# Quadrant products for the third batch of a fused attention and two-layer MoE kernel, with two engines' order written by hand from an earlier point

## The chip, the cores and the metric

One core of a Trainium2 chip runs the whole program. The metric is the device time of one execution in microseconds (us); lower is better. Where a median of runs is given, it is the median of three executions.

## The reference, cut to what matters

```python
attn_out = _attn_ref(q, k, v)                  # 4 batches, 8 heads, 576 tokens, head size 64; windows of 32 keys
x = attn_out.transpose(0, 2, 1, 3).reshape(4 * 576, 512)
h = np.maximum(np.maximum(x @ w1, x @ w2), x @ w3)   # 512 -> 768, three products and their maximum
x = h @ w_out                                         # 768 -> 512
logits = x @ w_gate                                   # gate, then a normalisation over tokens and experts
for e in range(8):
    out += P[:, e:e + 1] * (np.maximum(x @ w1[e], 0.0) @ w2[e])
```

Every product is done in float32 precision out of three passes: each operand is split into a high part and a low part (a copy on ScalarE, then a subtraction on VectorE or GpSimd), and high by high, low by high and high by low are summed.

## The kernel before, in words

The first half of the program works through the four batches (numbered 0 to 3). For each batch it does attention, then the "upper projections" (`x @ w1`, `x @ w2`, `x @ w3` and their maximum, rows 0 to 5 of the list `WORK`, as in "2.0" to "2.5"), then the lower projection ("2.out"). While TensorE multiplies for one batch, the attention of the next but one or next is slipped in. The list `WORK` is cut into units: six for each upper row, eight for each lower projection. Batch 1's rows 1.0 to 1.3 are units 56 to 79, "1.out" is 80 to 87, batch 2's rows are 88 to 123, "2.out" is 124 to 131 and batch 3's rows 132 to 167. After each unit `hooks(unit)` runs whatever the tables at the top of the file place there: `BEGIN` says in which unit each of four attention passes of a batch starts (each pass is two heads), and `LATE`, `PARTS` and `STAGES` say how many units later its steps come. Steps are named by letters: `S` the scores (TensorE), `Ma`, `Mb` the mask and the maximum (VectorE), `X` the exponentials (ScalarE), `Ra`, `Rb` the division (VectorE, then GpSimd), `T`, `E` the transposes and their evacuation, `V` the product with the values, `H`, `L` the evacuation of that product.

Upper projections come in two forms. `up` takes each of the 36 pieces of a batch (two halves of the 576 tokens, 18 column blocks) as 12 matmuls of 288 columns, 432 in all. `up_quads`, used for batch 3 alone, takes two column blocks and both token halves together as seven products of half the depth (Strassen's scheme in Winograd's form): nine such sets of 7 products of 6 matmuls, 378 in all. It needs sums of weight quadrants (`sums_w1`: four VectorE additions of 128x256 per set, fetched raw and stored to `wsf`), sums of the input's quadrants (`make_quad`: seven splits, four of them after a subtraction), and three more additions per set to put the results together (`result`). The sets go in groups of two; the fifth group has one.

The kernel keeps the split weights of the first two batches in DRAM (`wsp`), from where `up_quads` loads three quadrants as they are (`more_w1`, "A1" and "A2"); "S" loads the sums, "X" and "Y" split them.

What sets the order of instructions: TensorE's order is that of the code throughout. ScalarE's and VectorE's order is that of the code from "1.out" on, and before that a scheduler chooses it. GpSimd's and SyncE's order is the scheduler's. SyncE (SP) issues nearly all the DMAs, one after the other; each waits there until the buffer that it writes is free.

Of the kernel before, what the change touches and what calls it, by code (L numbers as in the profile page):

```python
# [9 lines left out]
F32 = mybir.dt.float32  # L10
# [7 lines left out]
B, H, S, D = 4, 8, 576, 64  # L18
# [5 lines left out]
    "2.0 2.1 2.2 2.3 2.4 2.5 2.out 3.0 3.1 3.2 3.3 3.4 3.5 3.out"  # L24
).split()

BEGIN = {2: (48, 60, 67, 71), 3: (91, 98, 105, 112)}
SUMS = (86, 89, 93, 96, 100, 103, 107, 110, 114)
WEIGHTS = 78
FIRST = {118: "S", 120: "A1", 121: "A2", 122: "X0", 123: "X1", 126: "Y0", 127: "Y1"}  # L30
LATE = {
    0: "S Ma", 1: "Mb", 2: "X0", 3: "X1", 4: "X2", 5: "X3", 6: "X4", 7: "Ra Rb", 8: "W",
    10: "T0 E0 T1 E1", 11: "T2 E2", 13: "V0 H0", 14: "V1 H1",
}
QUAD = {125: ("B11",), 126: ("T1",), 128: ("T2",), 129: ("B21",), 130: ("T3",), 132: ("B22",), 133: ("T4",)}
EARLY = {
    135: "X", 141: "d1", 143: "d3", 157: "d2", 159: "d4", 160: "w0", 165: "w1", 166: "A1.0", 167: "A2.0",
    168: "T2 s0", 169: "T1 S12.0", 170: "T3 S34.0", 171: "T4 A1.1", 172: "s1 A2.1", 173: "S12.1", 174: "S34.1",
}
PARTS = {  # L40
    0: "S Ma Mb X0", 1: "X1 X2", 2: "X3 X4 Ra Rb", 6: "W", 8: "T0 E0 T1 E1", 9: "T2 E2", 11: "V0 H0 L0 V1 H1 L1",
}
STAGES = {0: "S Ma Mb Xe Ra Rb", 6: "W", 8: "T0 E0 T1 E1", 9: "T2 E2", 11: "V0 H0 L0 V1 H1 L1"}


ORDER = (
# [25 lines left out]
P = 128  # L72
# [44 lines left out]
def attention_moe(ctx: ExitStack, tc: tile.TileContext, q, k, v, mask, wm1, wg, wm2, out):  # L117
# [64 lines left out]
    def attn_ops(b, p, pool, qt, kt):  # L182
# [146 lines left out]
            ops[f"T{g}"], ops[f"E{g}"] = partial(transpose, g), partial(evacuate, g)  # L329
        for a in range(2):  # L330
            ops[f"V{a}"] = partial(v, a)
            ops[f"H{a}"], ops[f"L{a}"] = (partial(hi, a), partial(lo, a)) if b < 3 else (partial(whole, a), list)
        return ops


# [33 lines left out]
    def w1_tile(g):  # L369
        if g < NG:  # L370
            return wa_p.tile([P, 2, 512], F32R, name="wa")
        return wb1_p.tile([P, 2, 512], F32R, name="wb1")

    def load_w1(g):
        raw = fetch_w1(g)
        ws = [w1_tile(g) for _ in range(2)]
        with tc.issue_after(final["Y"].ins):
            for i in range(2):
                split(nc, ws[i][:, 0], ws[i][:, 1], raw[:, i], nc.gpsimd)
                keep_w1(2 * g + i, ws[i])  # L380
        return ws
# [12 lines left out]

    def fetch(b, f):

        src = 0 if b == 1 and f >= NF1 - 2 else b
        while src == 1 and len(made[1]) < 3 * f + 3:
            made[1] += load_w1(len(made[1]) // 2)
        return made[src]  # L400
# [59 lines left out]
    stage, sums, raw_s, quads_w, best, raw_1 = [], {}, {}, {}, {}, {}  # L460
    groups = [[(3, i) for i in range(i0, min(i0 + 2, NQ1))] for i0 in range(0, NQ1, 2)]

    def fetch_next(g):
        raw_1[g] = fetch_w1(g)

    def split_next(j):
        t = w1_tile(j // 2)
        split(nc, t[:, 0], t[:, 1], raw_1[j // 2][:, j % 2], nc.gpsimd)
        made[2].append(t)

    def chunk(i, j):
        g = 3 * (2 * (i // 3) + j) + i % 3
        return wm1f[g // 2, :, g % 2]

    def fetch_sums(i):
        if i < 4 and i % 2 == 0:
            stage.append(cx_p.tile([P, 2, 2, 512], F32, name="stage", tag="cx"))
        raw = sums[i] = stage[i // 2 % 2][:, i % 2]
        for j in range(2):
            nc.sync.dma_start(raw[:, j], chunk(i, j))  # L480

# [54 lines left out]
    def make_quad(name):  # L536

        x = xf[3]
# [7 lines left out]
        t = quads_x[3, name] = quad(name)  # L546
        split(nc, t[:, 0], t[:, 1], o, nc.vector)

    def up_quads(g, unit):
# [13 lines left out]

        def product(k, side, w, x, first):
            if first:
                if side:
                    ps[k][side] = ps_a.tile([P, 512], F32, name="q", tag="pt", bufs=2)[:, :HB]
                else:
                    ps[k][side] = ps_g.tile([P, 512], F32, name="ps")[:, :HB]
            w, x = quads_w[group[k]][w], quads_x[b, x]  # L570
            n = 0
            for kk in range(2):
                for wi, xi in PASS:
                    nc.tensor.matmul(  # L574
                        ps[k][side], w[:, wi, kk], x[:, xi, kk], start=(first and n == 0),
                        stop=n == 5, skip_group_check=not first,
                    )
                    n += 1
# [18 lines left out]

        def after(n):
            nonlocal unit
            due = 7 * g + n + (n == 7 and g == len(groups) - 1)  # L600
            for _, op in [x for x in todo if x[0] < due]:
                op()
            todo[:] = [x for x in todo if x[0] >= due]
            n_done[0] = 7 * g + n + 1
            if n == 1:
                more_w1(g, "Y1") if g else None
                more_w1(g + 1, "S")
            for what in {2: ("A1",), 4: ("A2",), 5: ("X0",), 6: ("X1",), 7: ("Y0",)}.get(n, ()):
                more_w1(g + 1, what)
# [356 lines left out]
    def plan(b, p):  # L966

        if b < 3:
            return PARTS if p > 1 else STAGES
        return {i + (p == 1 and i > 12): names for i, names in LATE.items()}  # L970

    def hooks(unit):
# [19 lines left out]
        for what in FIRST.get(unit, "").split():
            more_w1(0, what)
        for late, step, op in ((0, 4, fetch_next), (4, 2, split_next)):
            i, now = divmod(unit - WEIGHTS - late, step)
            if 0 <= i < 36 // step and not now:
                op(i)
        for name in QUAD.get(unit, ()):
            make_quad(name)
# [13 lines left out]
    for what, unit in list(zip(WORK, starts))[done:]:  # L1013
        b, f = what.split(".")
        b = int(b)
        if what == "3.0":
            at_p.release()
            xs_p = tc.alloc_tile_pool(name="xs", bufs=1, side="right", reuse_waits="tile")
            sm_p = tc.alloc_tile_pool(name="sm2", bufs=1, side="right", reuse_waits="tile")
        if what == "1.out":  # L1020
            ordered.enter_context(tc.manual_schedule(engines={mybir.EngineType.Activation, mybir.EngineType.DVE}))
        if f == "out":
            down(b, unit)
            if b == B - 1:
                ordered.close()
        elif b == 3:
# [593 lines left out]
```

## Time and profile before

| | |
|---|---|
| median of 3 runs | 1840.87 us (1840.38 to 1847.17) |
| the profiled execution: its own time | 1839.86 us |
| the profiled execution: span from the first to the last instruction | 1838.1 us |
| TensorE (matmul) busy | 1823.5 us, 99% |
| VectorE, ScalarE, GpSimd busy | 1348.1, 961.8 and 602.6 us |
| DMA | 454.08 MB, 247 GB/s on average |

The profile was taken of one execution; its time lies 1.0 us under the median of the three runs. In the profile PE is TensorE's matmul stream, PEld its weight loads, DVE is VectorE, ACT ScalarE, POOL GpSimd, and SP SyncE. L425 is line 425 of the kernel before.

### The profile page before, as it was taken

How to read it: one execution, taken by the hardware profiler on the slowest of the kernel's cores; microseconds unless marked ns; L12 is line 12 of the kernel's file. 1: busy time of each engine (PE TensorE's matmuls, PEld its weight loads, DVE VectorE, ACT ScalarE, POOL GpSimd, SP SyncE). 2: the span in 40 equal slices, each digit the busy share in tenths (PEclk: the TensorE clock that was granted, in tenths of full speed). 3: DMA queues.
4: the chain of work that ended last, by engine and by line, in shares of the span. 5: the costliest groups of instructions: out<-in, count | busy, mean ns of one | idle time of the engine just before them, and what ended most of it. 6: DMA issues, size and time to landing. Idle time of an engine off the chain costs nothing.

```text
span 1838.1 us, 33541 instructions
## 1 busy us (share of the span) xinstructions
PE 1823.5 (99%) x11659; PEld 1703.1 (93%) x11659; DVE 1348.1 (73%) x2634; ACT 961.8 (52%) x2387; POOL 602.6 (33%) x536
## 2 busy tenths in 40 slices
PE   8999999999999999999999999999999999999999
PEld 6999999999999988899999999999999999999999
DVE  6884374768766677666597778877788777887777
ACT  6554454444554444544446555565555555565554
POOL 0013243336666677766512121121211211111211
PEclk8999999999999999999999999999999999999999
DMA  9678495866766678776977766777698676786773
GB/s 252 230 227 287 149 273 199 290 238 247 256 251 250 255 265 305 280 260 248 370 248 253 237 222 231 240 241 241 231 362 271 224 235 229 228 263 221 229 233 110
DMA packets 235369, 454.08 MB, mean 247 GB/s; under 512 B 38656, under 2 KB 121664, under 8 KB 233920
## 3 DMA queue, kind: packets, MB, share of 16 engines
q1 hardware_dynamic: 232240, 449.15, 72.4%
q10 hardware_dynamic: 2960, 2.79, 0.5%
q8 instruction: 93, 1.52, 0.3%
q14 instruction: 76, 0.62, 0.1%
HBM read 320.70 MB, written 130.81 MB: 246 GB/s over the span
## 4 chain that ended last, share of the span: by engine, by line
PE 75%; DVE 3%; DMA 1%; issue 1%; ACT 1%; POOL 1%; DVEq 0%; SPq 0%; POOLq 0%
PE po L1370 25%; PE po L1479 13%; PE po L1108 11%; PE p L1479 6%; PE q L1479 6%; PE p L1159 5%; PE q L1159 5%; PE ps L574 1%; DMA raw<-in_wm 1%; PE ps L652 1%; PE q L574 1%; DVE sums L839 1%; DVE ts L878 1%; DVE h L1212 1%; ACT h L1211 0%
## 5 line engine op out<-in xcount | busy, mean ns | idle before, releaser
L1370 PE MATMUL po<-wt,hop 128*128 128x512 f32 (+1 forms) x2772 | 469.7, 331 | 0.0
L1370 PEld LDWEIGHTS po<-wt,hop 128*128 128x128 f32 x2772 | 416.5, 188 | 51.0
L100 POOL TENSOR_TENSOR wt<-raw,wt 128x256 fp32r<-128x256 f32 x192 | 163.0, 874 | 757.8 <-ACT wt L99 677.1
L100 DVE TENSOR_TENSOR hop<-r,hop 128x384 fp32r<-128x384 f32 x384 | 210.5, 584 | 147.6 <-ACT hop L99 143.9
L1108 PE MATMUL po<-wb,h 128*128 128x512 f32 x1152 | 295.4, 392 | 0.4 <-POOL wb L100 0.4
L1108 PEld LDWEIGHTS po<-wb,h 128*128 128x128 f32 x1152 | 213.4, 188 | 33.9 <-POOL wb L100 1.0
L99 ACT CAST hop<-r 128x384 fp32r<-128x384 f32 x384 | 188.8, 516 | 50.0 <-DVE r L1346 28.2
L425 PE MATMUL ps<-xt,wa 128*128 128x288 f32 x1296 | 183.5, 298 | 0.0
L425 PEld LDWEIGHTS ps<-xt,wa 128*128 128x128 f32 x1296 | 173.5, 188 | 1.9
L100 POOL TENSOR_TENSOR wa<-raw,wa 128x256 fp32r<-128x256 f32 (+1 forms) x107 | 127.8, 1198 | 119.3 <-ACT wa L99 86.9
L1493 ACT ACTIVATE r<-r 128x384 f32<-128x384 f32 x192 | 97.8, 525 | 126.1 <-DVE r L1492 126.1
L1404 DVE SCALAR_TENSOR_TENSOR acc<-po,prob,acc 128x256 f32<-128x256 f32 x249 | 106.4, 478 | 17.3 <-PE po L1370 15.7
L100 POOL TENSOR_TENSOR tw<-ts,tw 128x512 fp32r<-128x512 f32 x64 | 87.2, 1382 | 91.7 <-DVE h L1212 59.1
L1479 PE MATMUL po<-xB,wa 128*128 128x384 f32 x576 | 115.5, 336 | 0.0
L1479 PE MATMUL po<-xt,wa 128*128 128x384 f32 x576 | 115.5, 336 | 0.0
L100 POOL TENSOR_TENSOR wa<-sums,wa 128x512 fp32r<-128x512 f32 x64 | 88.7, 1403 | 45.6 <-ACT wa L99 30.9
L1479 PEld LDWEIGHTS po<-xB,wa 128*128 128x128 f32 x576 | 101.3, 188 | 0.0
L1479 PEld LDWEIGHTS po<-xt,wa 128*128 128x128 f32 x576 | 101.3, 188 | 0.0
L100 POOL TENSOR_TENSOR wb<-raw,wb 128x512 fp32r<-128x512 f32 x64 | 93.0, 1453 | 23.7 <-ACT wb L99 23.2
L839 DVE TENSOR_TENSOR sums<-raw 128x256 f32<-128x256 f32 x64 | 46.3, 723 | 66.4 <-DMA raw<-in_wm 63.8
L1340 DVE TENSOR_TENSOR r<-r,r 128x384 f32<-128x384 f32 x128 | 93.2, 728 | 2.2
L1381 ACT COPY mm<-po 128x256 f32<-128x256 f32 x144 | 49.0, 376 | 73.5 <-PE po L1370 73.5
(239 smaller groups left out, 3318.6 us busy)
## 6 DMA issues: line engine op xcount, KB each, us to landing
wa<-wsd SPq DMA_DIRECT2D x192, 512.0 KB, 4.4
wt<-wtd SPq DMA_DIRECT2D x256, 256.0 KB, 3.6
wsd<-wa SPq DMA_DIRECT2D x96, 512.0 KB, 3.3
raw<-in_wm SPq DMA_DIRECT2D x64, 512.0 KB, 4.1
wtd<-tw SPq DMA_DIRECT2D x128, 256.0 KB, 2.7
raw<-in_wm SPq DMA_DIRECT2D x128, 256.0 KB, 5.2
wa<-wsd SPq DMA_DIRECT2D x64, 256.0 KB, 4.7
cx<-in_wm SPq DMA_DIRECT2D x10, 1024.0 KB, 7.2
```

Source lines behind the costliest of these rows:

```text
L99: nc.scalar.copy(hi, src)
L100: sub.tensor_tensor(out=lo, in0=src, in1=hi.bitcast(F32), op=ALU.subtract)
L425: nc.tensor.matmul(ps, w[:, wi, kk], xt[:, xi, kk, n0:n0 + HB], start=(n == 0), stop=(n == 3 * KT - 1),)
L839: nc.vector.tensor_tensor(out=s[:, o], in0=x, in1=y, op=op)
L1108: nc.tensor.matmul(po, self.hs[f, j][:, hi, t * P:(t + 1) * P], self.ws[f][:, wi], start=(n + f + k == 0), stop=(n == NPAIR - 1 and f == 1 ...
L1159: nc.tensor.matmul(ps, wo[w][:, wi, kk], xo[x][:, xi, kk], start=(first and k == 0), stop=True if k == 5 else False, skip_group_check=not ...
L1340: nc.vector.tensor_tensor(out=r[o, n], in0=r[x, n], in1=r[y, n], op=op)
L1370: nc.tensor.matmul(self.ps[side, t][:, 0:x.shape[-1]], h[:, hi, t * P:(t + 1) * P], x, start=(first and i == 0), stop=(n == NPAIR - 1 and ...
L1381: nc.scalar.copy(m, self.ps[ORD[k][0], t][:, 0:256])
L1404: nc.vector.scalar_tensor_tensor(out=a, in0=src, scalar=g, in1=a, op0=ALU.mult, op1=ALU.add)
L1479: nc.tensor.matmul(ps[k][side], wo[k][w][:, wi, kk], xo[x][:, xi, kk], start=(first and c == 0), stop=c == 5, skip_group_check=not first,)
L1493: nc.scalar.activation(out=r, in_=r, func=AF.Relu)
```

## The change

Batch 2's upper projections go through `up_quads` as batch 3's do. In `product`, batch 2 takes all its PSUM buffers from the pool `ps_g` (the banks that batch 3 uses for the second of its two sums hold attention work at that time), and starts its fourth product in the bank of the second. The weight sums are made earlier (`SUMS`: six of nine in batch 1's rows, three around "1.out" and the first units of batch 2), and are fetched three units ahead instead of five, into the ring of `raw` tiles instead of two `stage` tiles. Batch 1's own weights are loaded and split at units given by tables (`LOAD1`, `SPLIT1`) in place of when the product asks for them; the 18 weight tiles that were loaded and split for batch 2 go away. Batch 2's input is evacuated whole (`whole`) and split into quadrants at the units of `QUAD[2]`. The `STAGES` plan goes: batch 2's first two passes follow `LATE`. And the order of ScalarE and VectorE is that of the code from "0.out" on in place of "1.out".

```diff
-BEGIN = {2: (48, 60, 67, 71), 3: (91, 98, 105, 112)}
-SUMS = (86, 89, 93, 96, 100, 103, 107, 110, 114)
+BEGIN = {2: (48, 60, 68, 72), 3: (91, 98, 105, 112)}
+SUMS = (58, 61, 64, 67, 70, 73, 85, 88, 91)
+LOAD1 = (48, 50, 53, 58, 60, 65)
+SPLIT1 = (52, 53, 54, 56, 57, 58, 62, 63, 64, 68, 69, 70)
...
+    2: {80: ("B11",), 81: ("T1",), 84: ("B21",), 85: ("T2",), 86: ("T3",), 87: ("B22",), 88: ("T4",)},
...
-            ops[f"H{a}"], ops[f"L{a}"] = (partial(hi, a), partial(lo, a)) if b < 3 else (partial(whole, a), list)
+            ops[f"H{a}"], ops[f"L{a}"] = (partial(hi, a), partial(lo, a)) if b < 2 else (partial(whole, a), list)
...
+    def split_w1(j):
+        t = w1_tile(j // 2)
+        split(nc, t[:, 0], t[:, 1], raw_1[j // 2][:, j % 2], nc.gpsimd)
+        keep_w1(j, t)
+        made[1].append(t)
...
-        if i < 4 and i % 2 == 0:
-            stage.append(cx_p.tile([P, 2, 2, 512], F32, name="stage", tag="cx"))
-        raw = sums[i] = stage[i // 2 % 2][:, i % 2]
+        raw = sums[i] = raw_p.tile([P, 2, 512], F32, name="raw")
...
             if first:
-                if side:
+                if ps[k][side] is not None and b == 2:
+                    pass
+                elif side and b == 3:
                     ps[k][side] = ps_a.tile([P, 512], F32, name="q", tag="pt", bufs=2)[:, :HB]
...
+        if unit in SPLIT1:
+            split_w1(SPLIT1.index(unit))
+        if unit in LOAD1:
+            load_w1(LOAD1.index(unit))
         for i, u in enumerate(SUMS):
-            if unit == u - 5:
+            if unit == u - 3:
                 fetch_sums(i)
...
-        if what == "1.out":
+        if what == "0.out":
             ordered.enter_context(tc.manual_schedule(engines={mybir.EngineType.Activation, mybir.EngineType.DVE}))
```

SyncE before, around the start of batch 2's last attention pass (`kt` and `qt` are a pass's keys and queries, the first pair here those of that pass, the second those of batch 3's first; `vt` are values, `wsp` and `wm1f` weights in DRAM):

```order
L366 DMA raw<-wm1f 128x1024
L158 DMA kt<-in_k 128x608
L161 DMA qt<-in_q 64x9x64 x2
L166 DMA vt<-in_v 96x1152
L158 DMA kt<-in_k 128x608
```

SyncE now, at the same pass (the `raw` tiles of 128x512 are halves of two sets' raw weights, `wsf` takes a set's sums):

```order
L164 DMA kt<-in_k 128x608
L476 DMA raw<-wm1f 128x512 x2
L395 DMA wsp<-wa 256x1x256
L488 DMA wsf<-raw 128x1024
L476 DMA raw<-wm1f 128x512 x2
L167 DMA qt<-in_q 64x9x64 x2
L515 DMA wa<-wsp 128x1024 x2
```

Six transfers now stand between the keys and the queries of that pass, where none stood.

VectorE before, from the last evacuations of "1.out" into batch 2's first pieces (`x_2757` is the lower projection's output, `stage` the weight sums, `tmp` and `ps` the running maximum):

```order
L664 COPY x_2757<-ps 128x288 x4
L490 TENSOR_TENSOR stage<-stage 128x256 x2
L664 COPY x_2757<-ps 128x288
L490 TENSOR_TENSOR stage<-stage 128x256 x2
L438 TENSOR_TENSOR tmp<-ps,tmp 128x288
```

VectorE now, at the same place (`xf` are the input's quadrants being subtracted, `xt` their low halves being split, `raw` the weight sums, `best` the first results of batch 2's products):

```order
L541 TENSOR_TENSOR xf<-xf 128x2x288
L106 TENSOR_TENSOR xt<-xf,xt 128x576
L662 COPY x_2801<-ps 128x288
L106 TENSOR_TENSOR xt<-xf,xt 128x576
L486 TENSOR_TENSOR raw<-raw 128x256 x2
L541 TENSOR_TENSOR xf<-xf 128x2x288
L106 TENSOR_TENSOR xt<-xf,xt 128x576
L587 TENSOR_TENSOR best<-ps,tmp 128x288
```

The last evacuation of "1.out" and the first result of batch 2 now have weight sums, subtractions and splits of quadrants ahead of them.

## Rows read from the trace of the kernel before

**Rows 1.** The page: span, and busy time of each engine.
```profile
span 1838.1 us, 33541 instructions
PE 1823.5 (99%) x11659; PEld 1703.1 (93%) x11659; DVE 1348.1 (73%) x2634; ACT 961.8 (52%) x2387; POOL 602.6 (33%) x536
```

**Rows 2.** Windows: stretch, length; busy PE, PEld, DVE, ACT, POOL; clock, DMA share, GB/s.
```profile
154.40:204.50 50.10, 50.10 (x547) 48.61 (x546) 21.93 (x51) 25.12 (x95) 10.06 (x7) 1.00 0.54 173
204.50:227.00 22.50, 22.50 (x198) 22.26 (x197) 5.75 (x16) 7.13 (x19) 8.66 (x10) 1.00 0.64 216
227.00:299.50 72.50, 72.17 (x732) 69.56 (x730) 48.22 (x92) 38.03 (x135) 28.95 (x22) 1.00 0.82 253
```

**Rows 3.** Timeline of PE: start, us, instruction, count, idle before and its releaser.
```profile
179.03 1.86 PE L425 MATMUL ps<-xt,wa 128*128 128x288 f32 x12
...
186.59 1.27 PE L299 MATMUL pso<-pt,vt 96*64 96x64 f32 x36
187.78 1.04 PE L208 MATMUL pss<-kt,qt 64*64 64x96 f32 x36
...
276.16 1.34 PE L208 MATMUL pss<-kt,qt 64*64 64x96 f32 x36 [0.33 <-DMA qt<-in_q]
...
329.50 1.86 PE L574 MATMUL ps<-xt,wa 128*128 128x288 f32 x12 [0.45 <-ACT tmp L581]
...
344.49 3.34 PE L574 MATMUL ps<-xt,wa 128*128 128x288 f32 x24
347.67 1.76 PE L574 MATMUL q<-xt,wa 128*128 128x288 f32 x12
```

**Rows 4.** Timeline of DVE, in the columns of rows 3.
```profile
226.26 0.88 DVE L490 TENSOR_TENSOR stage<-stage 128x256 f32<-128x256 f32 x2
...
235.07 1.12 DVE L243 SCALAR_TENSOR_TENSOR sm<-pss,mk 128x480 f32<-128x480 f32 x2 [0.92 <-PE pss L208]
...
237.45 1.04 DVE L250 TENSOR_REDUCE st<-sm 128x9 f32<-128x864 f32 x1
...
259.16 2.00 DVE L490 TENSOR_TENSOR stage<-stage 128x256 f32<-128x256 f32 x2
...
321.40 0.74 DVE L545 TENSOR_TENSOR xf<-xf 128x576 f32<-128x576 f32 x1
322.89 0.76 DVE L100 TENSOR_TENSOR xt<-xf,xt 128x576 fp32r<-128x576 f32 x1 [0.74 <-ACT xt L99]
...
326.42 0.45 DVE L589 TENSOR_TENSOR best<-q,tmp 128x288 f32<-128x288 f32 x1
326.79 0.45 DVE L589 TENSOR_TENSOR best<-q,best 128x288 f32<-128x288 f32 x1
```

**Rows 5.** Lines by form of DVE, 150 to 400 us: busy us, mean ns, idle before.
```profile
L490 DVE TENSOR_TENSOR stage<-stage 128x256 f32<-128x256 f32 x36 | 25.1, 698 | 0.7
...
L593 DVE TENSOR_TENSOR best<-best 128x288 f32<-128x288 f32 x9 | 6.5, 727 | 0.3
```

**Rows 6.** Timeline of SP: start, us of issuing, transfer, count.
```profile
179.14 0.34 SPq L158 DMA_DIRECT2D kt<-in_k  x1
179.57 2.66 SPq L161 DMA_DIRECT2D qt<-in_q  x2
...
202.75 2.19 SPq L480 DMA_DIRECT2D stage<-wm1f  x4
```

**Rows 7.** Timeline of POOL, in the columns of rows 3.
```profile
228.09 0.80 POOL L100 TENSOR_TENSOR xg<-x,xg 128x288 fp32r<-128x288 f32 x1 [0.29 <-ACT xg L99]
...
259.58 1.29 POOL L100 TENSOR_TENSOR wa<-raw,wa 128x512 fp32r<-128x512 f32 x1 [1.29 <-issue]
```

**Rows 8.** DMA issues in 150 to 205 us: count, KB each, median us to landing.
```profile
qt<-in_q SPq DMA_DIRECT2D x6, 144.0 KB, 4.5
```

**Rows 9.** The instructions of tile qt, whole program: landing of its DMAs.
```profile
DMA to landing us min/median/max: 3.5/5.8/12.9
```

**Rows 10.** DMA issues in 230 to 300 us, in the columns of rows 8.
```profile
qt<-in_q SPq DMA_DIRECT2D x6, 144.0 KB, 7.1
```

More of the change, by code (lines that the diff above doesn't have):

```diff
@@ L25 @@
 ).split()
-BEGIN = {2: (48, 60, 67, 71), 3: (91, 98, 105, 112)}
-SUMS = (86, 89, 93, 96, 100, 103, 107, 110, 114)
-WEIGHTS = 78
-FIRST = {118: "S", 120: "A1", 121: "A2", 122: "X0", 123: "X1", 126: "Y0", 127: "Y1"}
+BEGIN = {2: (48, 60, 68, 72), 3: (91, 98, 105, 112)}
+SUMS = (58, 61, 64, 67, 70, 73, 85, 88, 91)
+LOAD1 = (48, 50, 53, 58, 60, 65)
+SPLIT1 = (52, 53, 54, 56, 57, 58, 62, 63, 64, 68, 69, 70)
+FIRST = {
+    0: {74: "S", 76: "A1", 77: "A2", 78: "X0", 79: "X1", 82: "Y0", 83: "Y1"},
+    5: {118: "S", 120: "A1", 121: "A2", 122: "X0", 123: "X1", 126: "Y0", 127: "Y1"},
+}
 LATE = {
@@ L34 @@
 }
-QUAD = {125: ("B11",), 126: ("T1",), 128: ("T2",), 129: ("B21",), 130: ("T3",), 132: ("B22",), 133: ("T4",)}
+QUAD = {
+    2: {80: ("B11",), 81: ("T1",), 84: ("B21",), 85: ("T2",), 86: ("T3",), 87: ("B22",), 88: ("T4",)},
+    3: {125: ("B11",), 126: ("T1",), 128: ("T2",), 129: ("B21",), 130: ("T3",), 132: ("B22",), 133: ("T4",)},
+}
 EARLY = {
@@ L40 @@
 PARTS = {
-    0: "S Ma Mb X0", 1: "X1 X2", 2: "X3 X4 Ra Rb", 6: "W", 8: "T0 E0 T1 E1", 9: "T2 E2", 11: "V0 H0 L0 V1 H1 L1",
+    0: "S Ma Mb X0", 1: "X1 X2", 2: "X3 X4 Ra Rb", 7: "W", 8: "T0 E0 T1 E1", 9: "T2 E2", 11: "V0 H0 L0 V1 H1 L1",
 }
-STAGES = {0: "S Ma Mb Xe Ra Rb", 6: "W", 8: "T0 E0 T1 E1", 9: "T2 E2", 11: "V0 H0 L0 V1 H1 L1"}
 ORDER = (
@@ L372, in w1_tile @@
         return wb1_p.tile([P, 2, 512], F32R, name="wb1")
+    raw_1 = {}
     def load_w1(g):
[L375 to L381, printed above, removed]
+        raw_1[g] = fetch_w1(g)
+    def split_w1(j):
[3 more added lines that the diff above has]
+        made[1].append(t)
     wsp = dram.tile([3 * NF1, P, 2, 512], F32, name="wsp")
@@ L395, in fetch @@
     def fetch(b, f):
[L397 to L400, printed above, removed]
+        return made[0 if b == 1 and f >= NF1 - 2 else b]
     def rows_in(b, f):
@@ L459, in attention_moe @@
     wsf = dram.tile([NQ1, P, 2, 512], F32, name="wsf")
[L460 to L469, printed above, removed]
+    sums, raw_s, quads_w, best = {}, {}, {}, {}
+    groups = [[(b, i) for i in range(i0, min(i0 + 2, NQ1))] for b in (2, 3) for i0 in range(0, NQ1, 2)]
+    NG1 = len(groups) // 2
     def chunk(i, j):
@@ L497, in more_w1 @@
     def more_w1(g, what):
-        group = groups[g] if g < len(groups) else ()
+        group = groups[g]
         if what[0] in "XY":
@@ L504, in more_w1 @@
             x = group[k]
-            row, names, sub = (0, ("S2", "S4"), nc.gpsimd) if what[0] == "X" else (1, ("S3", "S1"), nc.gpsimd if g in (2, 3) else nc.vector)
+            row, names, sub = (0, ("S2", "S4"), nc.gpsimd) if what[0] == "X" else (1, ("S3", "S1"), nc.gpsimd if g < NG1 or g % NG1 in (2, 3) else nc.vector)
             t = wa_p.tile([P, 2, 512], F32R, name="wa")
@@ L534, in quad, with make_quad @@
         return spaces[k][:, i:i + n].rearrange("p (s k n) -> p s k n", s=2, k=2)
-    def make_quad(name):
-        x = xf[3]
+    def make_quad(b, name):
+        x = xf[b]
         b11, b12, b21, b22 = (x[:, k:k + 2, n:n + HB] for k in (0, 2) for n in (0, HB))
@@ L545, in make_quad @@
             nc.vector.tensor_tensor(out=o, in0=y, in1=z, op=ALU.subtract)
-        t = quads_x[3, name] = quad(name)
+        t = quads_x[b, name] = quad(name)
         split(nc, t[:, 0], t[:, 1], o, nc.vector)
@@ L599, in after @@
             nonlocal unit
-            due = 7 * g + n + (n == 7 and g == len(groups) - 1)
+            due = 7 * g + n + (n == 7 and g % NG1 == NG1 - 1)
             for _, op in [x for x in todo if x[0] < due]:
@@ L605, in after @@
             if n == 1:
-                more_w1(g, "Y1") if g else None
-                more_w1(g + 1, "S")
+                more_w1(g, "Y1") if g % NG1 else None
+                more_w1(g + 1, "S") if (g + 1) % NG1 else None
             for what in {2: ("A1",), 4: ("A2",), 5: ("X0",), 6: ("X1",), 7: ("Y0",)}.get(n, ()):
-                more_w1(g + 1, what)
+                more_w1(g + 1, what) if (g + 1) % NG1 else None
             for _ in range((n + 1) // 2 - n // 2 if len(both) == 1 else 1 + (n == 7)):
@@ L968, in plan @@
         if b < 3:
-            return PARTS if p > 1 else STAGES
+            return PARTS if p > 1 else LATE
         return {i + (p == 1 and i > 12): names for i, names in LATE.items()}
@@ L991, in hooks @@
                 sums_w1(i, unit - u)
[L992 to L999, printed above, removed]
+        for g, when in FIRST.items():
+            for what in when.get(unit, "").split():
+                more_w1(g, what)
+        for b, when in QUAD.items():
+            for name in when.get(unit, ()):
+                make_quad(b, name)
         for what in EARLY.get(unit, "").split():
@@ L1025, in attention_moe @@
                 ordered.close()
-        elif b == 3:
+        elif b > 1:
             if f == "0":
```

## The prediction

> **What bounds the kernel now.** I read the page first: TensorE is busy 1823.5 of 1838.1 us, no other engine over 73% [rows 1]. The windows then say whether that holds where the change lies. In batch 1's upper rows, the lower projection and batch 2's upper rows PE is busy for 50.10 of 50.10, 22.50 of 22.50 and 72.17 of 72.50 us, at a granted clock of 1.00 (the 2.4 GHz level), while VectorE is at 44, 26 and 67% [rows 2]. So here the sum of TensorE's instructions is the time, and whatever else is added costs only what makes PE wait. The PE timeline names the two waits that the region has, 0.33 us at 276.16 (queries of an attention pass) and 0.45 at 329.50 [rows 3]; those 0.78 us are all that better cover could give.
>
> **What the matmuls give back.** Batch 2 goes from 432 to 378 matmuls of 288 columns, of the same shape, so 54 fewer. 24 in a row go by between the starts 344.49 and 347.67 [rows 3]: 3.18 us, 0.1325 us each. 54 x 0.1325 = 7.16 us, and PE has nothing to wait for instead as long as its operands come in time. Scores, transposes, values, gates and lower projections stay the same in number, so no other term falls.
>
> **The side engines' load.** In 2.x VectorE has 48.2 us of work in 72.5 [rows 2]. Add 27 additions at 0.45, 4 subtractions at 0.74 and 7 splits at 0.76 [rows 4], 20.4 us; take away six of the eight sets of weight sums that fall there before (SUMS lists units 89 to 114; now 88 and 91), 24 additions at 0.698 [rows 5], 16.8 us. That is 52 us in 72.5 - 7.2 = 65.3, or 80%, an upper bound, since most quadrants are made in 1.out and the old scheme's own maxima go. In 1.x it gets the six sets, 16.8 us on 21.9 of 50.1 [rows 2]: 77%. The weight splits for batch 2 are replaced by as many X and Y splits, so GpSimd's load hardly changes. Under PE's time, each costs nothing by its load; what counts is order, since ScalarE and VectorE now run exactly as the code is written from 0.out on. I find two places where order bites.
>
> **Place A: queries of batch 2's last pass (unit 72).** Call T the end of the third pass's score matmuls, 179.03 in the trace, when the next kt and qt buffers come free. The fourth pass's scores start at 187.78; the 1.19 us of value matmuls ahead of them (186.59 to 187.78 [rows 3]) now come behind, as the pass follows `LATE`, so PE wants the queries at T + 8.75 - 1.19 = T + 7.5. Before, SP issued kt at 179.14 and both qt from 179.57 on, in 2.66 us together [rows 6]. Now kt is followed by two raw fetches, which wait for a tile that GpSimd's split frees (1.29 us for one split [rows 7], so about T + 1.3), two stores, two more raw fetches, then qt. A raw fetch takes 2.19 / 4 = 0.55 us of issuing, kt 0.34 [rows 6]: 1.3 + 2 x 0.55 + 2 x 0.34 + 2 x 0.55 = T + 4.2, and the second qt's issue starts 0.55 (like a raw fetch) to 1.33 (half of 2.66) later; I take 0.65, T + 4.9. In this stretch a qt takes 4.5 us to landing [rows 8], so T + 9.4 and PE waits 1.9 us. Bounds: the quickest landing, 3.5 [rows 9], with a tile that is free at once (1.3 us less) gives no wait; 7.1, the median in 2.x [rows 10], gives 4.5. DMA rises in 1.x: six sets are fetched and stored, 2 x 128 x 1024 x 4 bytes each, 6.3 MB over 50.1 us on top of 173 GB/s, so about 299 GB/s, above 2.x's 253 [rows 2]. That speaks for a landing nearer 7.1; I still take 4.5, because the queries are the same pass's in the same stretch, and leave 7.1 to a rival.
>
> **Place B: from 1.out into 2.x.** Batch 2's first products write the banks that the last lower-projection outputs leave, and the bank of a product is freed by a copy or addition on VectorE that stands behind sums, subtractions and splits [the order of VectorE above]. A quadrant is a chain: subtraction 0.74, wait for ScalarE's cast 0.74, split 0.68 (0.76 less the overlap that starts show: results of 0.45 start 0.37 apart) [rows 4]. Three waits of PE follow, with s for one weight addition. (1) Last copy: from the copy before it, 0.37 + 2s + 2.16 + 0.37 = 2.9 + 2s of VectorE against 30 short PE instructions, 4.0 us. (2) First result: split 0.68, 2s, chain 2.16, result 0.45 = 3.3 + 2s, against 22 instructions, 2.9 us. (3) Second pair of results: two results, a maximum of 0.73 [rows 5], 4s, the mask of 1.12 and a result, 3.1 + 4s, against 36 matmuls, scores of 1.04 [rows 3] and a transpose, 5.8 to 6.3 us. Alone, two additions take 0.88 us, so s = 0.44; beside a GpSimd split of 1.29 (259.58 [rows 7]) two take 2.00, s = 1.00 [rows 4]; the mean of 36 is 0.70 [rows 5]. With s = 0.44 the waits are 0, 1.3, 0; with 0.70 they are 0.3, 1.8, 0.1; with 1.00, 0.9, 2.4, 1.3. So 1.3, 2.2 or 4.6 us. GpSimd splits the gate's inputs at this place (0.80 each [rows 7]), and not all the time: I take 2.2.
>
> The rows show two additions stretched by 1.12 us beside a split of 1.29, nearly the split's whole length. The Trainium skill, page "SBUF — State Buffer", section "Who interferes with whom", says that a VectorE instruction with two SBUF inputs contends with a GpSimd instruction that reads SBUF, and that the loser waits for the whole instruction; by that rule it would be the 4.6 wherever both run at once, and the trace agrees with it at 259.16.
>
> Beyond that, 1.x hides its sums beside PE time: a set of four there waits for its fetch on VectorE, with the masks of the third pass behind it; PE asks for their result in transposes ten units later, some 20 us at 50.1 / 24 a unit, so I price it at nothing.
>
> **Sum.** -7.16 + 1.9 + 2.2 = -3.1 us on the profiled 1839.86: 1836.8. The median of the runs lies 1.0 us above the profiled execution, so 1837.8.
>
> **Rivals.** B: both places are covered (the tile of place A is free earlier, GpSimd and VectorE don't meet) and the two old waits may go. 1840.9 - 7.16 = 1833.7, at best less 0.78, 1832.9. For it: bound 0 at place A, and each step of place B is a sum of worst starts. Against it: nothing in the trace shows (2) under 1.3.
>
> C, the other side: the queries land late because SP's queue holds them and DMA is busier. The wait is the landing less 2.6. At 7.1 it is 4.5, the sum -0.5, 1840.4: nothing gained. From 7.6 on (wait 5.0) the kernel is slower than before; at the longest landing of the trace, 12.9 [rows 9], the wait is 10.3 and the time 1846.2. To pass 0.5% it needs a wait of 14.2, so the longest landing and four more us that the tile's split is late, three GpSimd splits.
>
> D: at the boundary every addition meets a split: 4.6 in place of 2.2, 1840.2. For it, four additions in one window at 1.00; against it, additions at 0.44 in the last us of 1.out before [rows 4]. This is what the skill's section named above would make of every overlap.
>
> E: VectorE becomes the bound in 2.x. The 80% above is against it; it would need 13 us more work there, and then each us over costs one.
>
> **How the numbers follow.** Forecast as summed, with places A and B at 0 to 4.5 and 1.3 to 4.6 together not far from the values taken, 1835 to 1841: 0.45. B 0.23, C 0.15, D 0.10, E and mishaps 0.07. A measurement of this kernel can tell about 0.5%, 9.2 us, from no change: 1831.7 to 1850.1. Faster than that needs more than the matmuls and both old waits give (7.94): 0.06. Slower needs C at its extreme, or E: 0.07. Same: 0.87. The range reaches from B's best, 1832.9, to near C's longest landing: 1832.5 to 1845.5.
>
> **What would show it.** In the profile after: 378 matmuls of batch 2 at the same 0.1325 us; PE's waits in 1.x, one at the fourth pass's scores released by the DMA of qt, 1.9 us if I am right, none in B, over 4 in C; waits at the start of 2.x released by the last copy and the first result, 0.3 and 1.8; the weight additions there at 0.44 (B) or 1.00 (D); VectorE under 80% in 2.x. I am wrong if PE waits at a place I have not named: at weights from DRAM (A1, A2, sums) that come late with the fuller DMA, or at transposes whose division waits behind a weight sum.

## The result

The changed kernel takes 1850.63 us in the median of 8 runs (1849.02 to 1854.99), the kernel before 1840.62 (8 runs beside them, 1839.06 to 1847.17): ratio 1.0059, interval 1.0049 to 1.0069. It is slower by some 10 us, where 1837.8 was forecast and 1832.5 to 1845.5 given as the range. The profiled execution took 1850.65.

The page of the changed kernel says what [rows 1] said: PE at 99%, as busy in us as before although it has 54 matmuls less.

```profile
span 1848.9 us, 33530 instructions
PE 1823.4 (99%) x11605; PEld 1701.3 (92%) x11605; DVE 1368.1 (74%) x2658; ACT 972.4 (53%) x2412; POOL 602.6 (33%) x536
```

The windows of the three stages (columns of [rows 2]) say where the time went. 1.x runs from its first matmul to the first of 1.out, and 2.x from the last matmul of 1.out's lower projection to the first of 2.out; the expectations further down cut 1.x some 0.2 us earlier and so have 58.5 and 79.0 us:

```profile
151.00:209.30 58.30, 53.31 (x542) 50.55 (x540) 36.40 (x69) 26.90 (x98) 19.84 (x14) 0.94 0.98 317
209.30:232.30 23.00, 23.00 (x201) 22.55 (x199) 9.36 (x18) 9.04 (x25) 7.83 (x8) 1.00 0.64 203
232.30:311.10 78.80, 71.48 (x678) 67.86 (x678) 50.70 (x95) 46.66 (x156) 28.53 (x22) 0.91 0.72 228
```

In 1.x and 2.x PE stands still for 5.0 and 7.3 us, where it stood for 0 and 0.33, and its granted clock, 1.00 throughout these stages before, is 0.94 and 0.91. 1.x grew by 8 us, and 2.x, which should have lost 7, grew by 6. (The first 151 us were 3.4 us shorter in this one execution.) The DMA engines, half busy in 1.x before (0.54), are full there now (0.98, 317 GB/s). The list of PE's waits in the three stages (total, times, longest) names what ended each pause. `pst` are the attention's transposes, `sm` its divided scores, `best` the results of batch 2's products, `h` at L106 the split of a finished maximum, and `pg` the gate's products:

```profile
PE pst L290 <- ACT pt L293: 4.1, 1, 4.1
PE ps L572 <- DVE best L587: 3.6, 2, 2.5
PE ps L572 <- DVE h L106: 2.0, 1, 2.0
PE pg L703 <- ACT xg L105: 1.3, 1, 1.3
PE pst L290 <- POOL sm L280: 0.9, 1, 0.9
PE pg L703 <- POOL xg L106: 0.5, 1, 0.5
```

Now follow the largest one back. The timelines around the second pass's transposes, PE first, then DVE, ACT and SP:

```profile
176.56 1.04 PE L214 MATMUL pss<-kt,qt 64*64 64x96 f32 x36
...
181.90 0.86 PE L290 MATMUL pst<-ident,sm 128*96 128x128 f32 x6 [0.92 <-POOL sm L280]
182.51 1.82 PE L430 MATMUL ps<-xt,wa 128*128 128x288 f32 x12
188.41 0.88 PE L290 MATMUL pst<-ident,sm 128*96 128x128 f32 x3 [4.07 <-ACT pt L293]
188.94 3.23 PE L430 MATMUL ps<-xt,wa 128*128 128x288 f32 x12
```
```profile
178.11 1.63 DVE L486 TENSOR_TENSOR raw<-raw 128x256 f32<-128x256 f32 x2 [1.65 <-DMA raw<-wm1f]
179.66 0.17 DVE L276 TENSOR_SCALAR st<-st 128x9 f32<-128x9 f32 x1
179.86 0.21 DVE L277 RECIPROCAL st<-st 128x9 f32<-128x9 f32 x1
179.99 2.13 DVE L486 TENSOR_TENSOR raw<-raw 128x256 f32<-128x256 f32 x2
182.05 1.11 DVE L249 SCALAR_TENSOR_TENSOR sm<-pss,mk 128x480 f32<-128x480 f32 x2
```
```profile
184.41 0.37 ACT L269 ACTIVATE sm<-sm,st 128x96 f32<-128x96 f32 x1 [6.83 <-DVE st L256]
...
187.89 0.84 ACT L293 COPY pt<-pst 96x384 f32<-96x384 f32 x2
```
```profile
170.52 0.93 SPq L476 DMA_DIRECT2D raw<-wm1f  x1
...
183.82 1.36 SPq L167 DMA_DIRECT2D qt<-in_q  x2
```

Read from the bottom up. The raw weights of the fourth set come late: their two halves are issued from 170.52 on and take 6.0 and 6.5 us to landing. VectorE stops 1.65 us for them, and two pairs of additions take until 182.1. Behind these stand the third pass's mask, whose scores PE had ready at 177.6, and its maximum. ScalarE waits 6.83 us for that maximum, although nothing that PE needs at this point depends on it; behind its exponentials stands the evacuation of the second pass's transposes, and that frees the bank for which PE waits 4.07 us. SyncE's queue and the two that are in written order, VectorE's and ScalarE's, each stopped by its own first instruction, hand a late fetch on to TensorE. The pause of 0.92 us has a shorter path: the second pass's division (L276, L277, then GpSimd) stands behind the first pair of additions. The queries of place A were issued from 183.82 on, T + 6.3 instead of T + 4.2, and cost nothing: the pause ahead of them covered them.

At the start of 2.x it is the last set of sums (DVE, then PE):

```profile
247.22 2.02 DVE L486 TENSOR_TENSOR raw<-raw 128x256 f32<-128x256 f32 x2 [5.73 <-DMA raw<-wm1f]
249.16 1.11 DVE L249 SCALAR_TENSOR_TENSOR sm<-pss,mk 128x480 f32<-128x480 f32 x2
250.19 0.45 DVE L587 TENSOR_TENSOR best<-ps,tmp 128x288 f32<-128x288 f32 x1
```
```profile
250.69 1.99 PE L572 MATMUL ps<-xt,wa 128*128 128x288 f32 x12 [2.46 <-DVE best L587]
253.82 7.38 PE L572 MATMUL ps<-xt,wa 128*128 128x288 f32 x36 [1.14 <-DVE best L587]
```

VectorE stood 5.73 us for raw weights, with the result that frees PE's bank behind the additions. 36 matmuls that take 5.03 us elsewhere in 2.x then took 7.38.

**A second profile of each kernel** tells what of this is the kernel's and what is one execution's.

> The kernel before once more, for a second profile: how much its stretch ahead of batch 1's rows (154.2 us) and its stages (50.4, 22.2, 72.7 us) vary from execution to execution. If the stages agree within 0.3 us, differences of stages between kernels are theirs, and the spread of the runs comes from ahead of them.

> The changed kernel once more, for a second profile: the same pauses at the same instructions (0.92 and 4.07 us in 1.x, 2.46 and 1.14 and 1.98 in 2.x) within 0.5 us each, stages 58.5 and 79.0, if they come from the order of the instructions; other places and sizes if they come from chance in the DMA.

One run each: before 1837.84, changed 1849.44 us. Windows of the same stages, cut at the same matmuls, before, then changed:

```profile
154.20:204.30 50.10, 50.10 (x547) 48.61 (x546) 21.92 (x51) 25.12 (x95) 10.08 (x7) 1.00 0.54 173
204.30:226.70 22.40, 22.40 (x198) 22.16 (x196) 5.65 (x16) 7.13 (x19) 8.62 (x9) 1.00 0.64 218
226.70:298.60 71.90, 71.90 (x732) 69.48 (x731) 48.42 (x92) 38.06 (x135) 29.02 (x22) 1.00 0.84 255
```
```profile
154.90:212.10 57.20, 52.21 (x542) 49.58 (x540) 35.79 (x69) 26.90 (x98) 19.84 (x14) 0.97 0.98 317
212.10:235.10 23.00, 23.00 (x201) 22.56 (x199) 9.36 (x18) 9.23 (x26) 8.04 (x8) 1.00 0.69 219
235.10:309.70 74.60, 67.68 (x679) 64.11 (x678) 50.59 (x95) 46.30 (x156) 29.27 (x22) 0.98 0.77 240
```

The stages ahead of 2.x agree within 0.1 us in the kernel before, and 2.x within 0.7. PE's pauses come back at the same instructions in the changed one (0.92, 4.07, 2.46, 1.27 for 1.14, 1.98; the gate's inputs 1.2 in all for 1.7). They are the order's. What differs is mostly the clock behind them: 2.x is 4.2 us shorter at a clock of 0.98 than at 0.91. From these two profiles, 1.x costs 7.1 us, 1.out 0.6 (three more of the attention's transposes fall there) and 2.x 2.7: 10.4, the 10 us of the medians.

### The profile page after: what moved, and what is told of

It reads as the page before. It is cut to its first block, busy times and chain, and to the rows that moved or that the text cites. A ratio compares the mean times of both kernels' runs of the same rounds, so it can differ in the third digit from the quotient of the medians.

```text
span 1848.9 us, 33530 instructions
## 1 busy us (share of the span) xinstructions
PE 1823.4 (99%) x11605; PEld 1701.3 (92%) x11605; DVE 1368.1 (74%) x2658; ACT 972.4 (53%) x2412; POOL 602.6 (33%) x536
## 4 chain that ended last, share of the span: by engine, by line
PE 75%; DVE 3%; issue 1%; DMA 1%; ACT 1%; POOL 1%; DVEq 0%; SPq 0%; POOLq 0%
PE po L1370 25%; PE po L1479 13%; PE po L1108 11%; PE q L1479 6%; PE p L1479 6%; PE p L1159 5%; PE q L1159 5%; PE ps L572 1%; DMA raw<-in_wm 1%; PE ps L650 1%; PE q L572 1%; DVE sums L837 1%; DVE ts L876 1%; DVE h L1212 1%; ACT h L1211 0%
## 5 line engine op out<-in xcount | busy, mean ns | idle before, releaser
L106 POOL TENSOR_TENSOR wt<-raw,wt 128x256 fp32r<-128x256 f32 x192 | 163.0, 875 | 757.8 <-ACT wt L105 739.0
L106 DVE TENSOR_TENSOR hop<-r,hop 128x384 fp32r<-128x384 f32 x384 | 210.1, 582 | 147.5 <-ACT hop L105 147.5
L106 POOL TENSOR_TENSOR wa<-raw,wa 128x256 fp32r<-128x256 f32 (+1 forms) x107 | 127.4, 1192 | 145.6 <-ACT wa L105 125.3
L430 PE MATMUL ps<-xt,wa 128*128 128x288 f32 x864 | 123.6, 300 | 0.0
L430 PEld LDWEIGHTS ps<-xt,wa 128*128 128x128 f32 x864 | 117.0, 190 | 1.3 <-issue 0.2
L106 POOL TENSOR_TENSOR tw<-ts,tw 128x512 fp32r<-128x512 f32 x64 | 87.1, 1382 | 91.8 <-DVE h L1212 65.5
L106 POOL TENSOR_TENSOR wa<-sums,wa 128x512 fp32r<-128x512 f32 x64 | 88.0, 1393 | 45.6 <-ACT wa L105 27.9
L106 POOL TENSOR_TENSOR wb<-raw,wb 128x512 fp32r<-128x512 f32 x64 | 93.6, 1462 | 23.9 <-ACT wb L105 23.3
L572 PE MATMUL ps<-xt,wa 128*128 128x288 f32 x594 | 91.1, 308 | 6.0 <-DVE best L587 3.6
```

What stands on the lines that cost most here:

```text
L106: sub.tensor_tensor(out=lo, in0=src, in1=hi.bitcast(F32), op=ALU.subtract)
L430: nc.tensor.matmul(ps, w[:, wi, kk], xt[:, xi, kk, n0:n0 + HB], start=(n == 0), stop=(n == 3 * KT - 1),)
L572: nc.tensor.matmul(ps[k][side], w[:, wi, kk], x[:, xi, kk], start=(first and n == 0), stop=n == 5, skip_group_check=not first,)
```

## Experiments

Diffs are against the changed kernel. Ratios are to the kernel before, run beside each.

**Sums behind attention.** In `hooks` the loop over `SUMS` moves below the attention steps:

```diff
-            if unit in (u, u + 1):
-                sums_w1(i, unit - u)
...
                 for name in plan(b, p).get(i, "").split():
                     ahead[b, p][name]()
+        for i, u in enumerate(SUMS):
+            if unit in (u, u + 1):
+                sums_w1(i, unit - u)
```

> Only the place of the weight sums in VectorE's order changes: in each unit they come behind the attention steps, not ahead of them. Theory (VectorE's hand order puts a division and a mask of attention behind weight sums that wait for their fetch): the pauses at the transposes of batch 2's second pass (0.92 and 4.07 us) go, and with them the some 2.8 us lost to the half clock after them; the pauses at the start of 2.x stay. 1850.6 - 7.8 = about 1843. Rival (fetches come late, whatever stands behind them; SyncE is the cause): the wait for the fetch only moves to the next instruction of VectorE, under 2 us gained, 1849 or more.

1851.95 us, 1.0069 (1.0052 to 1.0086). The 0.92 went, the 4.07 became 3.28 and a third pause of 1.18 came up: the first pair of sums now let the division pass, but still stood (1.53 us for the fetch) ahead of the next unit's mask. The time is the rival's: here the order within a unit mattered little.

**Fetch five units ahead.** `unit == u - 3` becomes `unit == u - 5`.

> Weight sums' raw fetches are issued five units ahead of use instead of three, as before the change. Rival theory (late fetch): VectorE's two waits for raw weights (1.65 and 5.73 us) go, and with them the pauses of both places, 5.0 and 3.6 us, and about 6 us of half clock: about 1836. Theory of the ring (the four raw tiles are shared, so an earlier fetch only waits on SyncE for a tile, and holds queries and stores behind it): no gain, 1848 to 1856.

1847.73, 1.0046 (1.0031 to 1.0061). In 1.x the pauses stayed at 0.92 and 4.08. SP's timeline says why:

```profile
174.38 1.18 SPq L476 DMA_DIRECT2D raw<-wm1f  x2
```

The third pass's scores start at 180.79 here, so this fetch is issued 6.4 us ahead of them, against 6.0 (170.52 to 176.56) in the changed kernel. Asked for two units, some 4 us, earlier, it gained 0.4: the ring of four tiles holds it, as the theory of the ring had it. And it landed later: its halves took some 7.4 us, the same fetch in the changed kernel 6.0 and 6.5, and the five raw transfers ahead of that one in 1.x 4.4 to 5.3. VectorE waited 1.88 us instead of 1.65. While the fetch was on its way the DMA engines were busy all the time (by the profile's reckoning a share of 1.03 from 174.4 to 182.6, and 1.02 in the changed kernel from 170.5 to 178.1, where the kernel before had 0.51). So a late issue and a slow landing both have a part in the wait, and no run tells them apart. At the start of 2.x the fetch did come earlier: VectorE's wait of 5.73 us is gone there, the pauses of 3.6 us became one of 1.03, and 2.x came to 72.1 us. The median is below the changed kernel's, but the intervals of the two ratios overlap.

**Fetch with a buffer of its own.** The fourth and fifth set take a tile outside the ring, five units ahead:

```diff
+        if i == 3:
+            stage.append(cx_p.tile([P, 2, 2, 512], F32, name="stage", tag="cx"))
-        raw = sums[i] = raw_p.tile([P, 2, 512], F32, name="raw")
+        raw = stage[0][:, i - 3] if i in (3, 4) else raw_p.tile([P, 2, 512], F32, name="raw")
+        sums[i] = raw
```

> The fourth and fifth weight sums (units 67 and 70) get a buffer of their own outside the ring of four raw tiles, and are fetched five units ahead. Theory (the ring holds their fetch, the late fetch holds VectorE, that holds the mask, ScalarE and the transposes): VectorE's wait of 1.65 us for raw weights at that place goes, and the pauses of 0.92 and 4.07 us at the transposes shrink to at most 2 together, with less half clock: 1.x about 5 us shorter than the 58.5 of the changed kernel, 1845 to 1847. Rival (the additions themselves, not their wait, hold the mask): 1.x over 56 us, 1849 or more.

1850.13, 1.0053 (1.0035 to 1.0071). The fetch no longer holds VectorE; its additions and the exponentials remain (DVE, then PE):

```profile
181.70 0.87 DVE L489 TENSOR_TENSOR stage<-stage 128x256 f32<-128x256 f32 x2
...
182.82 1.80 DVE L489 TENSOR_TENSOR stage<-stage 128x256 f32<-128x256 f32 x2
184.54 1.11 DVE L249 SCALAR_TENSOR_TENSOR sm<-pss,mk 128x480 f32<-128x480 f32 x2
```
```profile
191.31 0.53 PE L290 MATMUL pst<-ident,sm 128*96 128x128 f32 x3 [2.71 <-ACT pt L293]
```

Of 4.99 us at the transposes 2.71 are left, so the late fetch made 2.3 of them. But the next scores now waited 1.09 us for a bank and 0.33 for queries, 1.x became only 2.0 us shorter (56.2), and the median did not move by what the runs can tell: the rival's case.

**Six sets moved.** `SUMS = (58, 61, 64, 75, 78, 82, 95, 98, 105)`; and, beside it, **the last three alone**, `(58, 61, 64, 67, 70, 73, 95, 98, 105)`.

> Six of the nine weight sums move: the fourth to ninth from units 67, 70, 73, 85, 88, 91 to 75, 78, 82, 95, 98, 105, behind the masks of batch 2's last two passes and away from the start of 2.x. Theory: the pauses at the transposes in 1.x and those on results at the start of 2.x go with their half clock; left are the waits on the gate's inputs (1.7 us), one of 2 us in the first group's last product, and perhaps the late queries forecast: 1836 to 1840. Rival (the hand order itself, or the boundary without sums): 1.x stays over 56 us or 2.x over 71, 1845 or more.

> The last three weight sums move from units 85, 88, 91 to 95, 98, 105, nearer to the places they had before the change. Theory (the last set's additions wait 5.73 us for their fetch and hold the results that free PE's banks): the pauses at 250.69 and 253.82 (2.46 and 1.14 us) and the half clock behind them (some 3.4 us) go, the pauses in 1.x stay: about 1843.6. Rival (the boundary is overfull without the sums too: casts, subtractions, splits): under 2 us gained, 1848 or more.

Six moved: 1843.43, 1.0018 (1.0007 to 1.0029), clearly below the changed kernel's 1.0059. 1.x fell from 58.3 to 51.9 us, its pauses to 0.74 and 0.55, and the results' pauses at the start of 2.x went. The third pass's mask now follows its scores at once, where it came 4.4 us behind them (window, DVE, PE):

```profile
156.30:208.20 51.90, 50.61 (x541) 48.12 (x539) 31.29 (x63) 26.77 (x98) 19.75 (x14) 1.00 0.96 305
```
```profile
182.90 1.12 DVE L249 SCALAR_TENSOR_TENSOR sm<-pss,mk 128x480 f32<-128x480 f32 x2 [0.86 <-PE pss L214]
```
```profile
189.23 0.53 PE L290 MATMUL pst<-ident,sm 128*96 128x128 f32 x3 [0.74 <-ACT pt L293]
```

The DMA engines are still full in 1.x here (0.96), so a full DMA alone does not make the pauses; the place of the sums does. The last three alone: 1847.62, 1.0045 (1.003 to 1.006), pauses of 1.x unchanged at 0.92 and 4.07, those on the first results gone. The pauses went as the theory had it, each place by its own sums; the times did not. Both runs are over what the theory forecast (1836 to 1840, and 1843.6) and over the kernel before, and the second is not told apart from the changed kernel. In both another pause of 2.5 us in 2.x remains, which waits for a maximum's split (the first of the two runs):

```profile
268.39 1.81 PE L572 MATMUL ps<-xt,wa 128*128 128x288 f32 x6 [2.50 <-DVE h L106]
```

**Order by the scheduler up to 1.out**, alone and with the six sets moved: `if what == "0.out":` becomes `if what == "1.out":`.

> The scheduler orders ScalarE and VectorE up to 1.out, as before the change; by hand only from there. Theory (hand order is what puts the division behind waiting sums): the scheduler lets other work pass, the pauses in 1.x go, the later ones stay: about 1843. Rival (fetch and traffic of the six sets that moved to 1.x): the pauses in 1.x stay, 1849 to 1853.

> The sums moved as in the run with six moved ones, and the scheduler orders ScalarE and VectorE up to 1.out. If hand order in 1.x costs something beyond the sums' place, this is faster than that run by over 2 us; by the theory it is the same within 2 us; if hand order is worth what it was made for, it is slower.

1855.71, 1.0087 (1.0072 to 1.0102) alone. With the six sets moved 1852.2, 1.007 (1.0053 to 1.0087), where the hand order had 1.0018. The hand order from 0.out on as such is not the fault; without it the kernel is slower in both cases. The first is over what both the theory and the rival forecast (1843; 1849 to 1853). The pauses at the transposes did fall, to 0.35 us in the first, so their path comes with the hand order. But a pause of 2.22 us on a copy by ScalarE came up ahead of 1.x (at 130.0 us; 1.65 in the second), and place A showed itself:

```profile
196.74 2.32 PE L214 MATMUL pss<-kt,qt 64*64 64x96 f32 x36 [3.56 <-DMA qt<-in_q]
```

**The remaining pauses, one after another**, each on top of the one before: the split of a maximum one product earlier (`todo.append((n_done[0] - (b == 2), ...))`), with the six sets moved; then `SUMS = (58, 61, 64, 74, 77, 90, 95, 98, 105)`; then batch 2's second pass at 59 instead of 60.

> The run with six moved sums, and the split of each finished maximum is written right behind the product that finishes it, one product earlier, so ahead of the next unit's exponentials in ScalarE's order. Theory (a PSUM bank of the first group is freed by that split, whose cast stands behind four exponentials): the pause of 2.5 us in 2.x and the some 2.9 us of half clock behind it go, 2.x from 74.3 to about 69: 1838 to 1839. Rival (ScalarE waits at the earlier place for the maximum and holds the same work): under 2 us gained, 1841.5 or more.

> As the run with the earlier split, and the set of sums at 82 moves to 90, with the two ahead of it one unit earlier, so that none of 1.out's units fetches or stores sums on SyncE. Theory (the stores of the gate's inputs stand on SyncE behind the sums' transfers, so that their two tiles come free late and PE waits 1.08 + 0.47 us for the last of them): those waits fall under 0.5, 1.1 us gained or more. Rival (the landing of the stores themselves, some 3 us at two tiles, sets it): they stay over 1 us.

> As the run with the cleared 1.out, and batch 2's second pass begins one unit earlier (59 in place of 60), so that its transposes are evacuated on ScalarE ahead of more of the third pass's exponentials. Theory (in ScalarE's hand order the third pass's exponentials stand ahead of the second pass's evacuations): the remaining pauses at transposes in 1.x (0.74 and 0.55 us) go, 1 to 1.5 us gained. Rival: they come from sums or weights and stay, same time within 1 us.

1843.83, 1.0029 (1.0017 to 1.004); 1841.22, 1.0018 (1.0009 to 1.0027); 1843.38, 1.0017 (1.0008 to 1.0026). The intervals do not tell the three apart. The pause on the split went, and one of 2.31 us at transposes came in its place, as the rival of the first had it (ACT, then PE, of the second):

```profile
258.34 0.43 ACT L105 CAST h<-tmp 128x288 fp32r<-128x288 f32 x1 [0.97 <-DVE tmp L591]
258.68 0.61 ACT L105 CAST wa<-raw 128x512 fp32r<-128x512 f32 x1
259.20 0.84 ACT L293 COPY pt<-pst 96x384 f32<-96x384 f32 x2
```
```profile
259.72 0.53 PE L290 MATMUL pst<-ident,sm 128*96 128x128 f32 x3 [2.31 <-ACT pt L293]
```

ScalarE waits 0.97 us for a maximum whose cast is not urgent, with an urgent evacuation behind it. The waits on the gate's inputs stayed at 0.59 + 0.48, mostly the rival's. With the second pass a unit earlier a pause of 1.16 at transposes stayed in 1.x, and the last pass's queries came 0.75 + 0.35 us late: the theory of that run fell.

**Attention steps ahead of the splits and loads in batch 2's products** (`hooks` called first in `after`), on top of the second of these.

> As the run with the cleared 1.out, but in batch 2 a unit's attention steps are written ahead of the splits and weight loads of that product, not behind. Theory (in 2.x ScalarE's order puts a cast that waits for VectorE's maximum ahead of the evacuation of transposes, and PE pauses there 2.31 and 1.96 us): these pauses fall under 1 us each, 2.x from 72.1 to about 69, total about 3 us less than that run. Rival (ScalarE and VectorE feed each other too tightly in 2.x, in any written order): the pause moves to another bank, 2.x stays over 71.

1842.91, 1.001 (0.9998 to 1.0023). The pauses of 2.31 and 1.96 went; five of 0.38 to 1.14 us came up, on results, on a weight split, on a maximum's split. 2.x came to 72.7, where the run that it builds on had 72.0: the rival's case.

**No sums at all**: the loop over `SUMS` in `hooks` is left out, and

```diff
-                nc.sync.dma_start(raw, wsf[i])
+                for j in range(2):
+                    nc.sync.dma_start(raw[:, j], chunk(i, j))
```

> The changed kernel without the 36 weight-sum additions, their fetches and stores: the later loads take raw weights in their place, so that part of the computation is left out. Theory (the additions and their fetches are the cause of the pauses in 1.x and at the start of 2.x): 1.x falls from 58.5 to about 52, 2.x from 79 to about 72, 1837 to 1840; what is left is the order of exponentials, casts and evacuations on ScalarE. If the sums are the whole cause, 1.x comes to 50.4 and 2.x to 66, about 1833. Rival (hand order without them too): over 1845.

1840.67 us, 0.9999 (0.9986 to 1.0011), in 10 runs from 1835.93 to 1843.28; the profiled one is the fastest of them. Its windows:

```profile
153.90:205.10 51.20, 50.46 (x542) 48.17 (x540) 20.93 (x45) 26.91 (x98) 19.54 (x14) 1.00 0.78 238
205.10:228.10 23.00, 23.00 (x203) 22.57 (x199) 8.76 (x15) 8.98 (x25) 7.87 (x8) 1.00 0.67 210
228.10:297.00 68.90, 65.57 (x679) 62.66 (x678) 46.18 (x86) 46.57 (x156) 28.78 (x22) 1.00 0.72 213
```

So the sums, that is their additions, fetches and stores together, are worth the 10 us between this and the changed kernel, and without them the change would have bought nothing that the runs can tell: the three stages come to 143.1 us against 144.4 of the second profile of before. 2.x is 68.9 at full clock, and PE stands 3.3 us in it (0.9 and 0.5 on the gate's inputs, 2.0 on the split of a maximum), so 65.6 of work and small gaps against 71.9: 6.3 of the 7.16 us.

**Sums on GpSimd** (`nc.gpsimd.tensor_tensor` in `sums_w1`), at the units of the changed kernel and at those of the cleared 1.out.

> The 36 weight-sum additions run on GpSimd in place of VectorE, at the units of the changed kernel. Theory (what costs is their place in VectorE's hand order, ahead of masks and results): the pauses at the start of 2.x (2.46 and 1.14 us) and most of that at the transposes in 1.x go, 1.x to about 53 and 2.x to about 70, 1841 to 1843. Rival (a GpSimd queue blocked by the same late fetch holds the division and the weight splits just as long): 1.x over 56, 1848 or more.

> The additions on GpSimd and six of the nine sets moved as in the run with the cleared 1.out (units 74, 77, 90, 95, 98, 105 for the last six). Theory: as without sums at all, 1.x about 51.5, 2.x about 69, the median near 1840.7 of the run that left them out. Rival (GpSimd's additions stretch VectorE's instructions with two SBUF inputs, or delay its splits): 2.x over 72, 1843 or more.

1848.24, 1.0043 (1.0026 to 1.0059), and 1849.36, 1.0048 (1.0033 to 1.0063). The pauses on VectorE's results did go in the first, and those at the transposes fell to 1.0 and 0.76 (1.x 55.1, 2.x 72.3), but PE waited 2.58 us in 1.x for values on a DMA, and 1.out grew from 23.0 to 24.6. In the second PE waited 2.4 us for a gate's input and 1.64 for a division, both on GpSimd, and 2.63 for an evacuation. The medians are the rivals'. That GpSimd hands the fetch and the additions on as VectorE did is seen in the second (that division stands behind an addition for which GpSimd waited 7.14 us, that gate's input behind 3.82 us of additions); for the first it isn't shown.

## Why the prediction was wrong

**The matmuls** were right: 54 fewer, and 6.3 us of 7.16 are seen in the run without sums.

**The step that failed** is the one that priced 1.x's sums at nothing ("a set of four there waits for its fetch on VectorE, with the masks of the third pass behind it; PE asks for their result in transposes ten units later"). It looked at the third pass's own transposes, and they were in time. It overlooked that ScalarE, now in written order too, waits for that mask's maximum with the second pass's evacuation behind it, which PE wants at once: 4.07 us. The second pass's division behind the same additions made 0.92 more. The term put at nothing was 4.99 us of pause, and 7.1 to 8.2 in 1.x with the clock behind it.

**Place B** was mis-sized, for the same reason: a fetch that is waited for. Waits (1) and (2), forecast at 0.3 and 1.8, are not there: the pairs of additions at that place took 0.87 and 0.88 us, so s was 0.44 and GpSimd was seldom in the way. Wait (3), forecast at 0.1, was 2.46, with one of 1.14 on the next result: I added up VectorE's work ahead of the result and left out that the second of its two pairs of additions waits 5.73 us for its fetch; that pair then took 2.02 instead of 0.88. Waits on the gate's inputs (1.7 us, 1.2 in the second profile) and on the maximum's split (1.98) weren't named.

**Place A**, forecast at 1.9, cost nothing in the changed kernel, because the pause ahead covers it. In other orders such a wait does come: 3.56 us where the scheduler's order took that pause away, and 1.1 in hand order with the second pass a unit earlier. In hand order with the six sets moved it is absent.

**The rivals.** Beside GpSimd's work pairs of additions took 1.63 and 2.13 us ahead of the third pass's mask and 2.02 ahead of the late result, where 0.88 is a pair's time alone. At waits (1) and (2) no pair met GpSimd's work, so rival D's sum did not come; but an estimated 2.0 us (0.75 + 1.25) of the mask's delay and 1.1 of the result's are this stretching. No run takes it away by itself. It agrees with the rule on the shared port in the Trainium skill's page "SBUF — State Buffer", section "Who interferes with whom". Rival C named the right kind, a transfer that SyncE's queue holds, and the wrong transfer. Rival E did not come: VectorE is busy 64% of 2.x. A kernel slower by over 0.5% was given a chance of 0.07, and only by C and E; it came by neither. The list of what would prove me wrong came near the cause, without a price: it has weights and sums "that come late with the fuller DMA", and "transposes whose division waits behind a weight sum". Part of the price was to be had: the six sets fill the ring of raw tiles that batch 1's weights share, and a fetch's distance in units says nothing if its tile isn't free.

**Half clock** had no term. In the changed kernel's first profile the clock was low at four places, each behind a pause.

What stays open: why thirteen orders and places of the same work end between 1.001 and 1.009 and none below 1. In the later ones each pause that went left another; that VectorE and ScalarE feed each other too tightly in 2.x fits this but isn't shown. Some of the rest lies ahead of the three stages: at some 111 us PE waits for values of an attention pass, 0.49 and 0 us in the two profiles before, 0 and 1.84 in those of the changed kernel, and 0.34 to 2.23 in twelve of the thirteen. Why these come late wasn't looked into.

## What to carry to other kernels

When an engine's order is fixed by hand, price each instruction by everything that stands behind it, on the engines that wait for that engine too: an instruction that nothing needs soon is harmful if it waits itself. Follow a chain of two or three in-order queues to the bound engine, and ask at each what is urgent behind the thing that isn't. A prefetch distance is only as long as the ring behind it: before counting on it, count the tiles in the ring and who else holds them, and ask how long a landing takes beside the traffic that the change adds.

## What was not expected of the hardware

TensorE at half clock (1.2 GHz) behind a pause, in one execution and not in another. After the pauses of 2.46 and 1.14 us the first profile of the changed kernel shows 0.50, the second, after 2.46 and 1.27 at the same instructions, 1.00 (windows, columns of [rows 2], first and second profile):

```profile
252.70:259.00 6.30, 5.18 (x21) 5.18 (x22) 2.68 (x6) 5.25 (x23) 2.18 (x2) 0.50 0.71 278
```
```profile
251.60:256.00 4.40, 3.13 (x22) 2.90 (x23) 4.18 (x10) 1.71 (x7) 0.01 (x1) 1.00 0.95 272
256.00:260.00 4.00, 4.00 (x45) 3.84 (x47) 1.37 (x3) 4.00 (x19) 2.57 (x2) 1.00 0.58 217
```

After the 4.07 us both fell, to 0.50 from 188.4 to 194.0 in the first, where 12 matmuls took 3.23 us instead of 1.82; in the second they took 3.06. Worked out from such windows, a pause of PE cost up to as much again in the work behind it: behind the gate's waits of 1.26 and 0.47 us the first profile has 4.0 us at a mean clock of 0.57, an estimated 1.7 us. How much is not the same from run to run.
